# Moving later decay scans, one load and one pair of a fused Mamba2 and FFN kernel to other places in its head

## The chip, the cores and the metric

One core of one Trainium2 chip. The metric is the device time of one execution in microseconds (us), taken as the median of several; lower is better. Fast runs of one kernel in the same rounds differ by up to 1.4% here, so kernels are compared through several fast runs of the same rounds. A run counts as slow, and is left out, when it is over 1.5% above the fastest of its kernel.

## The reference

A chunked linear attention (Mamba2-SSD) is followed by a bilinear feed-forward layer. Cut to what matters:

```python
# x: (4, 8, 768, 32)  a: (4, 8, 768)  B, C: (4, 8, 768, 16)
for c in range(nc):                                   # chunks along the sequence
    cum = np.cumsum(la, axis=-1)                      # la = log(a) of the chunk
    L = np.exp(cum[..., :, None] - cum[..., None, :]) * causal
    M = np.einsum('bhin,bhjn->bhij', Cc, Bc) * L
    y[:, :, sl] = M @ xc + (Cc @ state) * np.exp(cum)[..., None]
    state = decay_full * state + sum(Bc * xc * decay_from_j)
# ... then, with x = y as (3072, 256), w_a and w_b (256, 1536), w_out (1536, 256):
return ((x @ w_a) * (x @ w_b)) @ w_out
```

## The kernel before

The kernel works on blocks of 128 positions (not 32) and on two of the four batches at a time, which gives 12 "pairs" p. For each pair it does, in this order: scaling of B and C by decay factors; a transposition of both on TensorE (`transposes`); the scores C Bᵀ (`scores`); the causal mask (`mask`); the value product with x (`pv`), copied by ScalarE to `X2T`; then six "units" (p, k2) of the feed-forward layer and the output product. A unit is eight matmuls over 128x256, a sixth of the 1536 columns.

The decay factors come from scans on VectorE (running products of `a`, one of six blocks each), whose reciprocals are put into `selr`; small fp32 matmuls then spread them over the partitions (`factors_mm`, four calls for a block; the profile shows each as two matmuls, so eight for a block and 40 for five blocks).

```python
def load_w(q3, which=(0, 1)):                 # one third of Wa and/or Wb: pieces of 256 KB
    for W, src in [((Wa, moe_w_a), (Wb, moe_w_b))[w] for w in which]:
        c = slice(q3 * KC, (q3 + 1) * KC)
        wd.append(nc.gpsimd.dma_start(W[:, :, c], ...))
def warmup(n, bank, cols=512):                # matmuls whose result nobody reads
    for _ in range(n):
        nc.tensor.matmul(bank[:, 0:cols], warm[:, 0:128], warm[:, 0:cols], ...)
def unit(p, k2):
    a_ps = psf.tile([128, 512], f32, name="aps", tag="ff")     # psf: 4 PSUM banks
    b_ps = psf.tile([128, 512], f32, name="bps", tag="ff")
    ...                                                         # 8 matmuls
    nc.scalar.copy(asb, a_ps)
    return lambda: nc.vector.tensor_tensor(out=s["hk"]..., in0=b_ps, in1=asb, op=ALU.mult)
def go(*items):
    for p, k2 in items:
        unit(p, k2)()
# --- loads, in the order of SyncE's queue (B, C, x are numbers 0, 1, 2) ---
load1(nc.sync, 1, 0, 0)
load1(nc.sync, 1, 1, 1)
load1(nc.sync, 1, 0, 1)
load1(nc.sync, 1, 1, 0)
load1(nc.sync, 1, 2, 0)
load1(nc.sync, 1, 2, 1)
load(2)
# --- GpSimd's software queue: three weight pieces early ---
load_w(0)
...                                           # the causal mask
load_w(1, (0,))
# --- head ---
warmup(6, SC[3])
scan(0, 1)
sel_over_mid(0, 1)
v = factors_mm(0, 1)
...
transposes(0, [tb, tcp], nc.vector.tensor_copy, lambda: warmup(2, SC[3], 128))
scores(0)
...
load_w(1, (1,))                               # the fourth weight piece, after pair 0's GpSimd mask
load_w(2)
...
warmup(5, tcp)
pv_u(0, 0, py, True)                          # pair 0's value product in two halves
...
scan(3, NBLK)
h = unit(0, 0)
turn(0)                                       # pair 0's states
sel_over_mid(1, NBLK)
h()
go((0, 1))
v = factors_mm(1, NBLK)                       # 40 small matmuls
...
transposes(1, None, nc.vector.tensor_copy)
h = unit(0, 2)
scores(1)
mask(product(1, 3), by_pool=True)
mask(product(1, 2))
h()
h = unit(0, 3)
mask(product(1, 0))
scale_x(1, nc.scalar)
...                                           # gps: the products for the carried state
mask(product(1, 1))
h()
go((0, 4))
pv(1)
state(0)
state(1)
go((0, 5), (1, 0), (1, 1), (1, 2))
transposes(2)
go((1, 3))
h = unit(1, 4)
scores(2)
...
```

The schedule is manual: the profile shows the instructions of each engine in the order in which the program names them (on GpSimd the fourth weight piece is issued at 8.96 us, behind pair 0's mask at 7.86).

## Time and profile before

| | before |
|---|---|
| median of three runs | 130.52 us (130.06 to 130.95) |
| span of the profiled run | 128.0 us, mean granted TensorE clock 0.999 |
| TensorE busy | 118.6 us, 93% of the span |
| TensorE continuous | from about 25 us to the end, 9.03 us a pair |
| landing of pair 1's B and C, last halves | 11.8 and 12.3 us |
| landing of the fourth and last weight piece of Wa, Wb | 14.9 and 18.7 us |
| scores of pair 2 on TensorE | 26.93 us, with 11 units done |

To read it: in this kernel all work of TensorE from the scores of pair 2 onward is a fixed string without holes. So the start of those scores, put at equal work (0.87 us for each unit that is done more or less), is a gauge for the whole time. A matmul over 256 columns starts every 0.11 us at full clock (0.87 us for the eight of a unit, from 21.31 to 22.18 in the kernel before); in the timeline a group of four then spans 0.60 us.

### The profile page before, as it was taken

The page shows a single profiled execution, that of the slowest core. Times are in us where ns is not written, and L with a number is a line of the kernel's source. Part 1 is how long each engine was busy: PE and PEld are TensorE (multiplying, and loading weights), DVE is VectorE, ACT ScalarE, POOL GpSimd, SP SyncE. Part 2 cuts the span into 40 slices and gives each one's busy share as a digit, 9 for nine tenths or more (in the row PEclk, how much of TensorE's full clock was granted, in tenths as well). Part 3 has the DMA queues.
Part 4 walks back from the last instruction along what each step waited for, and adds up shares of the span by engine and source line. Part 5 has one row for each costly group of instructions (what it writes and reads, how often), then busy time and mean ns, then how long its engine had stood idle before and what let it go on. Part 6 is the DMA issues. An engine that isn't in the chain of part 4 may idle for free.

```text
span 128.0 us, 4399 instructions
## 1 busy us (share of the span) xinstructions
PE 118.6 (93%) x1761; PEld 97.1 (76%) x1761; DVE 89.6 (70%) x178; ACT 66.5 (52%) x129; POOL 62.0 (48%) x106
## 2 busy tenths in 40 slices
PE   6969979799999999999999999999999999999960
PEld 2425757688887888888888888888888888888840
DVE  4676769658695976967958959959759569364420
ACT  3344567594836545455556456465445464564410
POOL 7966830799982925907828447338339100000000
PEclk9999999999999999999999999999999999999999
DMA  3999999775435666566456555565565310211203
GB/s 66 158 215 164 211 199 216 117 136 111 105 67 88 156 90 111 120 110 142 91 96 146 104 87 131 111 111 123 101 133 116 73 42 0 46 41 23 51 8 82
DMA packets 51555, 13.76 MB, mean 107 GB/s; under 512 B 45328, under 2 KB 51504, under 8 KB 51536
## 3 DMA queue, kind: packets, MB, share of 16 engines
q1 hardware_dynamic: 46560, 10.72, 43.8%
q0 software_dynamic: 3184, 2.36, 12.5%
q10 hardware_dynamic: 1792, 0.41, 1.6%
q8 instruction: 13, 0.21, 0.7%
q14 instruction: 6, 0.05, 0.1%
HBM read 11.13 MB, written 3.15 MB: 111 GB/s over the span
## 4 chain that ended last, share of the span: by engine, by line
PE 77%; DMA 9%; SPq 7%; POOL 1%; issue 1%; ACTq 1%; DVE 0%; POOLq 0%
PE ops L493 25%; PE aps L476 22%; PE bps L476 21%; DMA cn<-in_C_dram 9%; SPq L123 7%; PE SC L380 3%; PE SC L336 3%; PE SC L397 2%; ACTq L123 1%; POOL bm L262 1%; PE SC L313 0%; POOL cm L262 0%; DVE osb L506 0%; POOLq L451 0%; POOLq L262 0%
## 5 line engine op out<-in xcount | busy, mean ns | idle before, releaser
L486 DVE TENSOR_TENSOR hk<-bps,asb 128x512 f16<-128x512 f32 x72 | 49.2, 687 | 20.8 <-ACT asb L485 18.9
L485 ACT COPY asb<-aps 128x512 f32<-128x512 f32 x72 | 42.1, 587 | 17.9 <-PE aps L476 16.4
L476 PE MATMUL bps<-X2T,Wb 128*128 128x256 f16 x288 | 43.2, 273 | 1.1 <-ACT G L611 1.1
L476 PE MATMUL aps<-X2T,Wa 128*128 128x256 f16 x288 | 43.5, 273 | 0.1
L493 PE MATMUL ops<-Wo,hk 128*128 128x256 f16 x288 | 35.3, 273 | 0.0
L476 PEld LDWEIGHTS <-Wb 128*128 128x128 f16 x288 | 28.1, 98 | 4.5 <-issue 0.6
L493 PEld LDWEIGHTS <-hk 128*128 128x128 f16 x288 | 27.4, 98 | 4.1
L476 PEld LDWEIGHTS <-Wa 128*128 128x128 f16 x288 | 26.8, 98 | 4.8 <-issue 0.3
L370 DVE TENSOR_TENSOR t<-SC,causal 128x512 f16<-128x512 f32 x45 | 29.4, 681 | 1.3 <-ACT tmp L367 1.0
L451 POOL TENSOR_TENSOR sbd<-U,maskbd 128x512 f16<-128x512 f32 x10 | 11.5, 1154 | 21.1 <-DVE U L447 21.0
L508 ACT ACTIVATE osb<-ops 128x256 f32<-128x256 f32 x23 | 8.8, 383 | 23.6 <-PE ops L493 22.9
L249 POOL TENSOR_SCALAR x<-xn 128x512 f16<-128x512 f32 x9 | 13.4, 1489 | 0.8 <-DMA xn<-in_x_dram 0.2
L408 ACT ACTIVATE X2T<-SC 128x512 f16<-128x512 f32 x11 | 6.6, 597 | 5.1 <-PE SC L380 5.1
L262 POOL TENSOR_TENSOR bc<-cn,fC 128x128 f16<-128x128 f32 x16 | 6.1, 402 | 5.6 <-DMA cn<-in_C_dram 3.4
L262 POOL TENSOR_TENSOR t<-bn,fB 128x256 f16<-128x256 f32 x12 | 7.7, 639 | 0.1
L262 POOL TENSOR_TENSOR bc<-bn,fB 128x128 f16<-128x128 f32 x16 | 6.1, 401 | 0.0
L380 PEld LDWEIGHTS <-x 64*32 64x32 f16 x384 | 3.2, 91 | 3.2 <-ACT x L247 1.6
L201 PE MATMUL SC<-warm 128*128 128x512 f16 (+1 forms) x14 | 4.4, 453 | 1.2 <-DVE warm L150 1.2
L427 DVE STREAM_TRANSPOSE dt<-SC 128x64 f32<-128x64 f32 x9 | 2.2, 249 | 4.1 <-ACT X2T L408 4.1
L262 POOL TENSOR_TENSOR cm<-cn,fC 128x128 f16<-128x128 f32 (+1 forms) x5 | 2.1, 445 | 5.9 <-DMA cn<-in_C_dram 5.9
L368 POOL TENSOR_TENSOR t<-tmp,causal 128x512 f16<-128x512 f32 x3 | 3.5, 1156 | 3.1 <-ACT tmp L367 3.1
L380 PE MATMUL SC<-t,x 64*32 64x144 f16 (+1 forms) x352 | 4.8, 224 | 0.0
(69 smaller groups left out, 66.8 us busy)
## 6 DMA issues: line engine op xcount, KB each, us to landing
xn<-in_x_dram SPq DMA_DIRECT2D x23, 128.0 KB, 3.2
out_dram<-osb SPq DMA_DIRECT2D x46, 64.0 KB, 2.1
bn<-in_B_dram SPq DMA_DIRECT2D x23, 64.0 KB, 2.7
cn<-in_C_dram SPq DMA_DIRECT2D x23, 64.0 KB, 3.3
Wa<-in_moe_w_a_dram POOLq DMA_DIRECT2D x3, 256.0 KB, 6.8
Wb<-in_moe_w_b_dram POOLq DMA_DIRECT2D x3, 256.0 KB, 6.6
Wo<-in_moe_w_out_dram POOLq DMA_DIRECT2D x1, 768.0 KB, 10.2
xn<-in_x_dram ACTq DMA_DIRECT2D x1, 128.0 KB, 5.4
```

The costliest lines, as they stand in the source:

```text
L123: return eng.dma_start(pair_in[p][which][64 * bt : 64 * bt + 64].rearrange("i h r n -> i h (r n)"), src.rearrange("h (i r) n -> i h (r n)" ...
L249: eng.tensor_scalar(xo, xi, XS, None, ALU.mult)
L262: return eng.tensor_tensor(out=out, in0=i0, in1=i1, op=ALU.mult)
L370: nc.vector.tensor_tensor(out=o_, in0=i_, in1=c_, op=ALU.mult)
L380: nc.tensor.matmul(py[bt][32 * g : 32 * g + 32, u * (Q + N) : u * (Q + N) + w], s["X16"][k, h, r, :], s["T1"][k, h, r, 0:w], start=(first ...
L408: nc.scalar.activation(out=X2T[:, p].rearrange("p u t q -> p t u q"), in_=s["PY"][:, :, :, 0:Q], func=AF.Copy, scale=YS / XS,)
L451: nc.gpsimd.tensor_tensor(out=Sbd.rearrange("p t (h d) -> p t h d", h=H), in0=U32[:, p].unsqueeze(2).broadcast_to((128, 2, H, D)), in1=mas ...
L476: nc.tensor.matmul(ps[:, kk * 2 * Q : (kk + 1) * 2 * Q], W[:, f, k * 128 : (k + 1) * 128], X2T[:, p, f].rearrange("p t q -> p (t q)"), sta ...
L485: nc.scalar.copy(asb, a_ps)
L486: return lambda: nc.vector.tensor_tensor(out=s["hk"][:, 2 * k2 : 2 * k2 + 2, :].rearrange("p k q -> p (k q)"), in0=b_ps, in1=asb, op=ALU.mult)
L493: nc.tensor.matmul(o_ps[:, 0:d_model], hk[:, k, bt * Q : (bt + 1) * Q], Wo[:, k, :], start=(k == 0), stop=(k == NK - 1), skip_group_check= ...
L508: nc.scalar.activation(out=o_sb, in_=o_ps[:, 0:d_model], func=AF.Copy, scale=1.0 / (YS * YS))
```

## The change

Its intent is to take the waits of the head away. Three parts:

1. **Scans and factors early.** The scans of blocks 1 to 5 move ahead, and the 40 factor matmuls go into places where TensorE waited or ran warm-up matmuls: 16 between pair 0's transposes, 24 before pair 0's value product. Five of 23 warm-ups go (two of 128 columns, three of 512). Scaling pair 1's C goes from GpSimd to VectorE, some memsets change engines. Three small products for the carried state (`hr`, `hs`, `hsx`) and one `selr` go from VectorE to GpSimd, a copy of pair 0 from VectorE to ScalarE, and the causal mask is made ahead of the first weight piece.
2. **Loads.** The fourth weight piece is issued directly behind the third. x of pair 1 leaves SyncE's queue for GpSimd's software queue: one half behind the fourth weight piece, one ahead of the last two.
3. **Pair order.** Pair 1's value product and units (1,0) to (1,3) run ahead of (0,4) and (0,5), which need the last weights. The matmul `gps` for the carried state moves behind (1,0).

```diff
-    load1(nc.sync, 1, 2, 0)
-    load1(nc.sync, 1, 2, 1)
...
+    load_w(0)
+    load_w(1)
+    load1(nc.gpsimd, 1, 2, 0)
...
-    transposes(0, [tb, tcp], nc.vector.tensor_copy, lambda: warmup(2, SC[3], 128))
-    scan(2, 3)
+    transposes(0, [tb, tcp], None, lambda: factors_mm(fps[:, W1 : 3 * W1], 1, 3))
+    scan(3, NBLK)
...
-    load_w(1, (1,))
+    load1(nc.gpsimd, 1, 2, 1)
     load_w(2)
-    scale_bc(1, 1, nc.gpsimd)
...
-    warmup(5, tcp)
+    warmup(1, tcp)
+    factors_mm(fps3[:, 0 : 3 * W1], 3, NBLK)
+    warmup(1, tcp)
...
-    scan(3, NBLK)
     h = unit(0, 0)
     turn(0)
-    sel_over_mid(1, NBLK)
     h()
+    scale_bc(1, 1, nc.vector)
     go((0, 1))
-    v = factors_mm(1, NBLK)
...
-    go((0, 4))
     pv(1)
+    turn(1)
+    go((1, 0))
+    ...                                       # gps and its copy
+    go((1, 1))
     state(0)
     state(1)
-    go((0, 5), (1, 0), (1, 1), (1, 2))
+    go((1, 2), (1, 3))
     transposes(2)
-    go((1, 3))
-    h = unit(1, 4)
+    go((0, 4))
+    h = unit(0, 5)
     scores(2)
```

More of the change, by code (lines that the diff above doesn't have):

```diff
@@ L146 @@
     load1(nc.sync, 1, 1, 0)
-    load1(nc.sync, 1, 2, 0)
-    load1(nc.sync, 1, 2, 1)
     load(2)
     nc.vector.memset(warm.bitcast(u32), 0)
+    nc.vector.memset(headm, 1.0)
     nc.vector.memset(zero, 0.0)
-    for t_ in bc:
-        nc.vector.memset(t_[:, 0:4].rearrange("p k h n -> p (k h n)").bitcast(u32), 0)
+    nc.vector.memset(ident, 1.0)
+    nc.vector.memset(causal, 1.0)
     nc.gpsimd.memset(sel, 1.0)
@@ L163 @@
     )
-    nc.gpsimd.memset(headm, 1.0)
     for sign, base in ((1, 0), (-1, N - 1)):
@@ L177 @@
     )
-    nc.gpsimd.memset(ident, 1.0)
     nc.gpsimd.affine_select(
@@ L188, in load_w @@
             wd.append(nc.gpsimd.dma_start(W[:, :, c], src.rearrange("(f p) e -> p f e", p=128)[:, :, c]))
-    load_w(0)
-    nc.gpsimd.memset(causal, 1.0)
     for bt in range(2):
@@ L196 @@
         )
-    load_w(1, (0,))
+    load_w(0)
+    load_w(1)
+    load1(nc.gpsimd, 1, 2, 0)
     def warmup(n, bank, cols=512):
@@ L208, in scan, with sel_over_mid @@
             nc.vector.tensor_tensor_scan(Pr[:, k], a_sb[:, k], zero, 1.0, ALU.mult, ALU.add)
-    def sel_over_mid(lo, hi):
+    def sel_over_mid(lo, hi, eng=None):
         nc.vector.reciprocal(rmid[:, lo:hi], Pr[:, lo:hi, 63])
-        nc.vector.tensor_tensor(
+        (eng or nc.vector).tensor_tensor(
             out=selr[:, lo:hi].rearrange("p k t c -> p k (t c)"),
@@ L217, in sel_over_mid, with factors_mm @@
         )
-    def factors_mm(lo, hi):
-        fps = psf.tile([128, 512], f32, name="fps", tag="ff")
-        F = fps[:, 0 : (hi - lo) * 2 * NBP * H].rearrange("p (k r c) -> p k r c", k=hi - lo, r=2)
+    def factors_mm(fps, lo, hi):
+        F = fps.rearrange("p (k r c) -> p k r c", k=hi - lo, r=2)
         for k in range(lo, hi):
@@ L233, in factors_mm @@
                     )
-        return F.rearrange("p k r c -> p (k r c)")
     def flat(f, lo, hi):
@@ L537 @@
     sel_over_mid(0, 1)
-    v = factors_mm(0, 1)
-    nc.vector.reciprocal(flat(fB, 0, 1), v)
-    nc.scalar.copy(flat(fC, 0, 1), v)
+    W1 = 2 * NBP * H
+    fps = bank("fps")
+    factors_mm(fps[:, 0:W1], 0, 1)
+    scan(1, 3)
+    nc.vector.reciprocal(flat(fB, 0, 1), fps[:, 0:W1])
+    nc.scalar.copy(flat(fC, 0, 1), fps[:, 0:W1])
     warmup(2, SC[3])
@@ L543 @@
     scale_bc(0, 0, nc.vector)
+    sel_over_mid(1, 3)
     n1 = scale_bc(0, 1, nc.vector)
-    scan(1, 2)
     tb, tcp = bank("tb"), bank("tc")
-    transposes(0, [tb, tcp], nc.vector.tensor_copy, lambda: warmup(2, SC[3], 128))
-    scan(2, 3)
+    transposes(0, [tb, tcp], None, lambda: factors_mm(fps[:, W1 : 3 * W1], 1, 3))
+    nc.scalar.copy(flat(fC, 1, 3), fps[:, W1 : 3 * W1])
+    scan(3, NBLK)
     warmup(1, SC[3])
@@ L553 @@
     tc.add_manual_dep(n0.ins, n1.ins.name, AFTER, reason="C first")
+    sel_over_mid(3, NBLK, nc.gpsimd)
     mask(product0(1, 1), by_pool=True)
@@ L565 @@
     nc.gpsimd.tensor_copy(maskbd, headm.unsqueeze(2).broadcast_to((128, H, D)))
+    for t_ in bc:
+        nc.gpsimd.memset(t_[:, 0:4].rearrange("p k h n -> p (k h n)").bitcast(u32), 0)
     n0 = load(3)
     tc.add_manual_dep(n0[0].ins, wd[5].ins.name, AFTER, reason="weights first")
-    warmup(5, tcp)
+    fps3 = bank("fps")
+    warmup(1, tcp)
+    factors_mm(fps3[:, 0 : 3 * W1], 3, NBLK)
+    nc.scalar.copy(flat(fC, 3, NBLK), fps3[:, 0 : 3 * W1])
+    warmup(1, tcp)
     py = st[0]["py"] = [bank("py0"), bank("py1")]
@@ L579 @@
     warmup(1, tcp, 128)
-    scan(3, NBLK)
     h = unit(0, 0)
     turn(0)
-    sel_over_mid(1, NBLK)
     h()
+    scale_bc(1, 1, nc.vector)
     go((0, 1))
-    v = factors_mm(1, NBLK)
-    nc.vector.tensor_tensor(out=hr, in0=Pr[:, 0:NG, Q - 1], in1=rmid[:, 0:NG], op=ALU.mult)
-    nc.vector.tensor_tensor(out=hs, in0=hr, in1=Pr[:, 1:NBLK, 63], op=ALU.mult)
-    nc.vector.tensor_tensor(
-        out=hsx,
-        in0=hs.unsqueeze(1).broadcast_to((BH, nb, NG)),
-        in1=selb.rearrange("p (b g) -> p b g", b=nb),
-        op=ALU.mult,
-    )
     transposes(1, None, nc.vector.tensor_copy)
-    nc.scalar.copy(flat(fC, 1, NBLK), v)
     h = unit(0, 2)
@@ L606 @@
     load(4)
+    mask(product(1, 1))
+    h()
+    nc.gpsimd.tensor_tensor(out=hr, in0=Pr[:, 0:NG, Q - 1], in1=rmid[:, 0:NG], op=ALU.mult)
+    nc.gpsimd.tensor_tensor(out=hs, in0=hr, in1=Pr[:, 1:NBLK, 63], op=ALU.mult)
+    nc.gpsimd.tensor_tensor(
+        out=hsx,
+        in0=hs.unsqueeze(1).broadcast_to((BH, nb, NG)),
+        in1=selb.rearrange("p (b g) -> p b g", b=nb),
+        op=ALU.mult,
+    )
+    scale_bc(2, 1, nc.gpsimd)
+    scale_bc(2, 0, nc.gpsimd)
+    tail(2, nc.gpsimd)
+    pv(1)
+    turn(1)
+    go((1, 0))
     gps = bank("gps")
@@ L611 @@
     nc.scalar.copy(G.rearrange("p b g -> p (b g)"), gps[:, 0 : nb * NG])
-    mask(product(1, 1))
-    h()
-    scale_bc(2, 1, nc.gpsimd)
-    scale_bc(2, 0, nc.gpsimd)
-    tail(2, nc.gpsimd)
-    go((0, 4))
-    pv(1)
+    go((1, 1))
     state(0)
     state(1)
-    go((0, 5), (1, 0), (1, 1), (1, 2))
+    go((1, 2), (1, 3))
     transposes(2)
-    go((1, 3))
-    h = unit(1, 4)
+    go((0, 4))
+    h = unit(0, 5)
     scores(2)
@@ L628 @@
     scale_x(2, nc.scalar)
-    h2 = unit(1, 5)
+    h2 = unit(1, 4)
     mask(product(2, 1))
+    h()
     mask(product(2, 2))
-    h()
+    h2()
+    go((1, 5))
     out_half(0, 0)
-    h2()
     scale(3)
```

## The prediction

> **What bounds the kernel now.** I read the page's busy slices first, then the chain that ended last, then the four-window table, and only then the PE timeline of the head. The slices:
>
> ```profile
> PE   6969979799999999999999999999999999999960
> DMA  3999999775435666566456555565565310211203
> PE 77%; DMA 9%; SPq 7%; POOL 1%; issue 1%; ACTq 1%; DVE 0%; POOLq 0%
> ```
>
> A slice is 3.2 us. TensorE has holes only in the first eight slices and the last two; the DMA engines are full in slices 2 to 7. The chain is loads for its first part and TensorE afterwards. The window table (core; us, then busy us and instructions of each engine, clock, DMA) says the same in numbers:
>
> ```profile
> 0.00:10.80 10.80, 8.16 (x99) 3.62 (x100) 5.87 (x18) 4.10 (x9) 8.47 (x22) 1.00 0.93 153
> 10.80:25.10 14.30, 11.95 (x189) 9.28 (x188) 11.61 (x30) 7.96 (x17) 6.59 (x12) 1.00 1.24 183
> 25.10:123.60 98.50, 98.48 (x1479) 84.16 (x1476) 71.74 (x131) 54.22 (x104) 46.93 (x74) 1.00 0.47 94
> ```
>
> From 25.10 to 123.60 us PE is idle for 0.02 us. In the chain, the first 12-matmul group of a pair starts at 62.07, 71.10, 80.12, 89.15 and 98.18: 9.03 us a pair. So whatever the change does, it can only pay in the head, by letting PE do more of its fixed work before the place where it becomes continuous. The head on PE (start, busy us, operation, count, wait):
>
> ```profile
> 10.82 0.80 PE L476 MATMUL aps<-X2T,Wa 128*128 128x256 f16 x4
> 12.17 0.60 PE L476 MATMUL aps<-X2T,Wa 128*128 128x256 f16 x4
> 13.21 1.38 PE L225 MATMUL fps<-selr,Pr 32*64 32x16 f32 x40
> 16.17 0.43 PE L336 MATMUL SC<-ct,bt 32*64 32x128 f16 x32 [0.38 <-DVE ct L323]
> 17.86 0.60 PE L476 MATMUL aps<-X2T,Wa 128*128 128x256 f16 x4
> 19.52 0.60 PE L476 MATMUL bps<-X2T,Wb 128*128 128x256 f16 x4 [1.06 <-ACT G L611]
> 20.05 0.45 PE L380 MATMUL SC<-t,x 64*32 64x144 f16 x32
> 24.86 0.28 PE L313 MATMUL SC<-ident,bm 128*128 128x128 f16 x2 [0.77 <-POOL bm L262]
> 26.93 0.43 PE L336 MATMUL SC<-ct,bt 32*64 32x128 f16 x32
> ```
>
> I call the eight matmuls of one pair and one sixth of the columns a unit; (0,4) is pair 0, sixth 4. Units (1,0), (1,1), (1,2) start at 21.31, 22.18, 23.05: 0.87 us each. Time lost between 10.82 and 25.10: about 0.5 before (0,1) at 12.17 (its bank is held until VectorE turns pair 0's states, which stands behind three scans, 10.98 to 12.01); 1.4 for the 40 factor matmuls; 0.5 before pair 1's scores at 16.17; 1.2 inside (0,4) between 18.30 and 19.52; 0.9 before pair 2's transposes at 24.86. Sum 4.5 us. That is the most that the change can win here.
>
> [...] So I use start spacing. [...] 0.87 us / 8 = 109 ns. [...] loads of x issued at 7.9 to 10.3 us land 7.2 and 9.1 us later, where the shortest of that kind takes 2.9. So putting x of pair 1 on GpSimd's queue changes its place, not its cost.
>
> **The change part by part.** Durations are those of the rows of before.
>
> 1. *Scans and factor products.* 16 of the 40 factor matmuls go between pair 0's transposes, 24 before pair 0's value product. PE runs warm-up work or waits there now: it waits 1.13 us until 9.41 for x of pair 0, whose scaling starts on ScalarE at 8.72. 24 x 34.5 ns = 0.83 us. GpSimd makes their weights after VectorE's last early reciprocal, near 7.7, so they run about 8.1 to 8.9. This just fits. The cost: scans, reciprocals and selr delay pair 0's masks by some 0.5 us (VectorE 7.21 to 7.75, done 9.65), but the first product needs only two of the three, done near 9.05. As the weights' issue starts 0.7 us later (masks are made first), x of pair 0 may come a little earlier. I put unit (0,0) at 10.6, before 10.82. The scans being gone from 10.98, (0,1) follows directly, near 11.6 to 12.5, before 12.17 to 13.04. With the factor products gone, transposes of pair 1 may start at 12.6, before 14.52. Gain so far 1.9 us.
>
> 2. *Pair 1's C on VectorE.* Scaling C (0.41 us) moves behind pair 0's first product hk (0.65 us from 11.95): 12.6 to 13.0. GpSimd does B right after the weights' issue, 11.8 to 12.5; B's last half landed at 11.8, C's at 12.3 before. So C's transposes start near 13.05: 0.3 us lost on PE. Then two ScalarE copies (0.84), one VectorE copy (0.29): scores of pair 1 near 14.15, if unit (0,2) between them is not held up.
>
> 3. *Weights.* Landings of the six weight pieces before: 8.1, 9.8, 12.0, 14.9, 16.8, 18.7 (issue plus time to landing); 1.7 to 2.2 us apart except where the fourth was issued only at 8.96. Now four are issued back to back from about 3.0: estimated 8.5, 10.3, 12.3, 14.2. (0,2) wants the fourth at 13.6. I charge 0.5 us: scores at 14.7. Then x of pair 1: two pieces of 128 KB, an estimate of about 1 us each, so 16.3, before 18.7.
>
> 4. *Pair 1 ahead of the last weights.* Scores to value product took 16.17 to 20.05 before, and VectorE's part (wait for ScalarE's tmp, mask, hk, two masks) ends at 19.85 whatever PE does. The same row of VectorE stands in the changed order, so 3.7 us again: value product at 18.4. But now PE has only (0,3) to do in it: 0.37 + 0.87 us. A **new hole of about 2.5 us**. After the value product PE wants pair 1's X2T at once: 0.15 + 0.60 + 0.05 us after its 0.37, another hole of 0.8; before, (0,5) ran there. So (1,0) starts at 18.4 + 0.37 + 0.8 = 19.6. Then (1,0), gps (0.3), (1,1) to (1,3) until 23.4, transposes 0.23, (0,4) and (0,5) until 25.4, scores of pair 2. The wait for the last weights (18.7 before, now about 20, wanted at 23.6) is gone. The wait for C of pair 2 is gone as well: SP has two loads fewer ahead of it, so it should land near 17, before 23.2.
>
> *Sum.* Scores of pair 2: 25.4 with 10 units done; before 26.93 with 11. At equal work 25.4 + 0.87 = 26.3, a gain of 0.65 us; 1.15 if the fourth weight piece is not waited for. Removed 4.5 + 0.2, newly lost 0.3 + 0.5 + 2.5 + 0.8 = 4.1. All behind it is continuous PE work and keeps its 98.5 us.
>
> **Rivals.** *All of it is won.* If the two new holes were filled, the gain would be 3.5 to 4 us: 126.5 to 127. For it: all four old waits are really attacked. Against: in the changed order no PE work stands between (0,3) and the value product, nor between that and (1,0). *Loads eat it.* The weights now share one first-in, first-out queue with x; if x of pair 1 lands after 18, or the fourth weight piece after 15, each us later costs one us: 130.5 to 131.5. For it: the DMA engines are full until 23 us and the bytes stay the same. Against: x had 2.4 us to spare in my row, and C of pair 2 leaves the path. *VectorE becomes the bound* after pair 1, with four state updates of 0.19 us between hk's: at 0.7 us per hk against 0.87 per unit it catches up; 0.3 us at most. *The clock halves* in the 2.5 us hole: [...] I see no sign of it in the trace with 1.1.
>
> **Range and chances.** 130.5 - 0.8 (between 0.65 and 1.15) = 129.7. The three runs before spread 0.9 us. Both holes filled by luck of earlier landings would give 128.6; late loads 130.7. Over 2% needs 2.6 us of the 4.7 at stake, and the 3.3 us of structural holes stand against that: 0.04. Slower by 2% needs a late load chain of over 3 us: 0.02.
>
> **What would show it.** Right: no factor matmuls after 10 us; (0,1) directly behind (0,0); pair 1's scores at 14 to 15; a PE hole of 2 to 2.5 us before pair 1's value product, ended by VectorE's mask, and one of 0.8 behind it, ended by ScalarE's X2T; no PE wait for weights after 20 or for C of pair 2; continuous PE with the same 9.03 us a pair; a span near 127.2. Wrong: the hole ended by DMA x or ScalarE x, unit (0,2) waiting over 1 us for the fourth weight piece, or the hole much shorter because pair 1's masks come faster than 3.7 us after its scores.

## The result and the profile after

The changed kernel takes **135.01 us** (134.31 to 136.96, four runs) against 130.74 us (130.06 to 131.14, four runs) for the one before. The ratio is 1.032, with a 95% interval from 1.025 to 1.039: slower, outside the predicted range. A ratio here always compares the fast runs of two kernels from the same rounds, so it is not quite the ratio of the medians. One of the changed kernel's runs was slow and is not in the ratio.

The page of the changed kernel, with the busy tenths of TensorE, its granted clock in tenths, and the engines' shares of the chain that ended last:

```profile
PE   6897195899999999999999999999999999999970
PEclk9999757779999999999999999999999999999999
DMA  3899999864038467555645646557555420120213
PE 77%; DMA 10%; DVE 5%; ACT 2%; issue 1%; ACTq 1%; SPq 0%; DVEq 0%
```

A slice is 3.3 us. Before, the clock row was 9 throughout; now it drops in slices 5 to 9 and TensorE is almost idle in slice 5, where it had been at 9. Behind slice 9 all is as it was. The window table has, after the window, its length and then busy us (and instructions) of TensorE, weight loads, VectorE, ScalarE and GpSimd, the granted clock, the DMA share and GB/s:

```profile
10.80:25.10 14.30, 8.70 (x110) 5.65 (x109) 6.18 (x14) 5.47 (x10) 7.92 (x17) 0.76 1.29 192
17.00:19.00 2.00, 2.00 (x26) 1.22 (x32) 0.88 (x3) 1.43 (x3) 1.40 (x4) 0.50 1.23 206
25.20:28.20 3.00, 3.00 (x15) 2.09 (x15) 1.60 (x5) 0.90 (x3) 0.00 (x0) 0.50 0.50 104
```

Between 10.8 and 25.1 us TensorE did 110 matmuls in 8.70 busy us; before it did 189 in 11.95. Two stretches have exactly half the clock while TensorE is busy without a break. The timeline of TensorE (start, us, operation, count, and the idle time before it with what ended it) names the places:

```profile
10.58 0.80 PE L471 MATMUL aps<-X2T,Wa 128*128 128x256 f16 x4
11.65 0.60 PE L471 MATMUL aps<-X2T,Wa 128*128 128x256 f16 x4
15.90 0.40 PE L308 MATMUL SC<-ident,bm 128*128 128x128 f16 x2 [3.21 <-POOL bm L257]
16.79 0.39 PE L308 MATMUL SC<-ident,cm 128*128 128x128 f16 x2 [0.49 <-DVE cm L257]
16.97 1.06 PE L471 MATMUL aps<-X2T,Wa 128*128 128x256 f16 x4
18.82 0.65 PE L331 MATMUL SC<-ct,bt 32*64 32x128 f16 x32
22.19 0.24 PE L375 MATMUL SC<-t,x 64*32 64x144 f16 x4 [0.91 <-POOL hsx L605]
22.70 0.43 PE L375 MATMUL SC<-t,x 64*32 64x144 f16 x28 [0.26 <-DVE t L365]
23.84 0.60 PE L471 MATMUL aps<-X2T,Wa 128*128 128x256 f16 x4 [0.71 <-ACT X2T L403]
26.92 1.06 PE L471 MATMUL aps<-X2T,Wa 128*128 128x256 f16 x4
31.44 0.43 PE L331 MATMUL SC<-ct,bt 32*64 32x128 f16 x32
```

Up to 12.5 us this is what was predicted: (0,0) at 10.58, (0,1) at 11.65, no factor products between. Then pair 1's transposes wait 3.21 us for B, whose scaling on GpSimd had itself waited for its load; what follows runs at half clock (1.06 us for four matmuls at 16.97). The value product is at 22.70, then comes the hole of 0.71, and unit (1,2) at 26.92 is at half clock again. The hole of 0.91 is put down to `hsx` on GpSimd, but VectorE's mask of the first heads ended within 0.1 us of it (21.37 plus half of 1.28 us for two): the releaser is inferred, and the mask is as likely.

The time can be added up at equal work in this one profiled run, against the run before. The first step also contains the first stretch at half clock, from about 14.5 to 21.5 us, whose own cost no run separates:

| place | before | after | step |
|---|---|---|---|
| value product of pair 1 (its main part) | 20.05 | 22.70 | +2.65 |
| units of pair 0 done by then | 5 | 4 | +0.87 |
| hole behind it | none | 0.71 | +0.71 |
| half clock behind it | none | about 3.4 us | about +1.7 |
| wait for pair 2's B and C | 0.77 | none | -0.77 |
| sum of the rows above | | | +5.2 |
| scores of pair 2, at equal work | 26.93 | 31.44 + 0.87 | +5.38 |

The 1.7 is from this trace: (1,0) to (1,3) with `gps` took 5.53 us (23.84 to 29.37), where four units of 0.87 and 0.35 for `gps` make 3.83. The spans differ by 5.5 us (133.5 and 128.0). So three things have to be explained: the late B and C, the holes, and the half clock. The DMA queues from 8 to 12 us (packets, MB, share of 16 engines' time; q0 is the software queue with the weights, q1 SyncE's), before:

```profile
DMA packets 2625, 0.72 MB, mean 181 GB/s; under 512 B 2189, under 2 KB 2625, under 8 KB 2625
q0 software_dynamic: 468, 0.45, 78.4%
q1 hardware_dynamic: 2156, 0.28, 50.8%
```

And after:

```profile
DMA packets 1596, 0.84 MB, mean 210 GB/s; under 512 B 896, under 2 KB 1590, under 8 KB 1596
q0 software_dynamic: 739, 0.74, 107.9%
q1 hardware_dynamic: 857, 0.11, 28.4%
```

More bytes moved, but SyncE's queue, with B and C of pair 1, got 857 small packets in place of 2156. Their last halves landed at 15.2 and 15.9 us; the prediction had taken over 11.8 and 12.3.

### The profile page after: what moved, and what is told of

It is laid out like the page before. It is cut to its first block, busy times and chain, and to the rows that moved or that the text cites.

```text
span 133.5 us, 4393 instructions
## 1 busy us (share of the span) xinstructions
PE 121.6 (91%) x1756; PEld 98.8 (74%) x1756; DVE 89.6 (67%) x177; ACT 67.1 (50%) x131; POOL 63.9 (48%) x110
## 4 chain that ended last, share of the span: by engine, by line
PE 77%; DMA 10%; DVE 5%; ACT 2%; issue 1%; ACTq 1%; SPq 0%; DVEq 0%
PE ops L488 24%; PE aps L471 22%; PE bps L471 22%; DMA cn<-in_C_dram 10%; PE SC L375 3%; PE SC L331 3%; DVE hk L481 2%; PE SC L392 2%; DVE t L365 1%; ACT asb L480 1%; DVE U L440 1%; DVE cm L257 1%; ACTq L123 1%; ACT x L242 0%; PE SC L308 0%
## 5 line engine op out<-in xcount | busy, mean ns | idle before, releaser
L471 PE MATMUL aps<-X2T,Wa 128*128 128x256 f16 x288 | 45.3, 281 | 0.7 <-ACT X2T L403 0.7
L471 PE MATMUL bps<-X2T,Wb 128*128 128x256 f16 x288 | 44.9, 280 | 0.4 <-ACT asb L480 0.4
L471 PEld LDWEIGHTS <-Wb 128*128 128x128 f16 x288 | 29.0, 101 | 4.6 <-issue 0.5
L471 PEld LDWEIGHTS <-Wa 128*128 128x128 f16 x288 | 27.6, 100 | 5.8 <-issue 0.9
L446 POOL TENSOR_TENSOR sbd<-U,maskbd 128x512 f16<-128x512 f32 x10 | 11.6, 1156 | 23.8 <-DVE U L442 19.6
L503 ACT ACTIVATE osb<-ops 128x256 f32<-128x256 f32 x23 | 8.8, 384 | 24.5 <-PE ops L488 22.9
L244 POOL TENSOR_SCALAR x<-xn 128x512 f16<-128x512 f32 x9 | 13.4, 1491 | 2.6 <-DMA xn<-in_x_dram 2.1
L198 PE MATMUL SC<-warm 128*128 128x512 f16 (+1 forms) x12 | 3.9, 472 | 1.3 <-DVE headm L149 1.3
L317 ACT ACTIVATE bt<-SC,par 128x256 f16<-128x256 f16 x6 | 2.5, 471 | 4.4 <-PE SC L308 4.3
## 6 DMA issues: line engine op xcount, KB each, us to landing
xn<-in_x_dram SPq DMA_DIRECT2D x21, 128.0 KB, 3.5
xn<-in_x_dram POOLq DMA_DIRECT2D x2, 128.0 KB, 8.4
```

Source lines behind the costliest of these rows:

```text
L244: eng.tensor_scalar(xo, xi, XS, None, ALU.mult)
L446: nc.gpsimd.tensor_tensor(out=Sbd.rearrange("p t (h d) -> p t h d", h=H), in0=U32[:, p].unsqueeze(2).broadcast_to((128, 2, H, D)), in1=mas ...
L471: nc.tensor.matmul(ps[:, kk * 2 * Q : (kk + 1) * 2 * Q], W[:, f, k * 128 : (k + 1) * 128], X2T[:, p, f].rearrange("p t q -> p (t q)"), sta ...
L503: nc.scalar.activation(out=o_sb, in_=o_ps[:, 0:d_model], func=AF.Copy, scale=1.0 / (YS * YS))
```

## The experiments

Fifteen kernels; all gave the right result. Each has its own runs of the kernel before in the same rounds. The questions were: does the fourth weight piece or x of pair 1 delay B and C; what does the clock cost; what does each of the three parts do alone; what do the dropped warm-ups do.

### The fourth weight piece late (a_w1b_late)

```diff
 # against the changed kernel
-    load_w(1)
+    load_w(1, (0,))
     load1(nc.gpsimd, 1, 2, 0)
...
+    load_w(1, (1,))
     load1(nc.gpsimd, 1, 2, 1)
```

> The changed kernel with one edit: the fourth weight piece (Wb, second third) is issued after pair 0's GpSimd mask, as before the change, instead of straight behind the third. Theory A ([...] B and C of pair 1 land at 15.2 and 15.9 us instead of 11.8 and 12.3): they land before 13.5 us, the 3.2 us TensorE hole before pair 1's transposes shrinks under 1 us, the first half-clock stretch goes, time 129.5 to 131.5. Rival B (B and C are late because SP's own later loads were issued earlier, or because of x of pair 1 in the software queue): they still land after 15 us, time 134 to 136.

Theory A was that the early fourth piece on the software queue makes B and C of pair 1 late; rival B, that SyncE's own later loads or x of pair 1 do. 133.27 us; ratio to before 1.0246 (1.0186 to 1.0306), against 1.0319 for the changed kernel. B and C landed at 13.2 and 13.7. TensorE's timeline:

```profile
13.89 0.28 PE L308 MATMUL SC<-ident,bm 128*128 128x128 f16 x2 [1.02 <-POOL bm L257]
16.10 0.61 PE L471 MATMUL bps<-X2T,Wb 128*128 128x256 f16 x4 [1.19 <-DMA Wb<-in_moe_w_b_dram]
```

The wait for B falls from 3.21 to 1.02 us, and 1.19 comes back as a wait for the very piece that was postponed. In these two profiles the early fourth piece makes up 2.0 of the 3.4 us that B came later, and 2.2 of the 3.6 for C; it is not the reason for most of the loss. The time lies above theory A's range. Landings scatter: the six profiles of kernels of this family with the piece early have B at 13.6 to 15.2 us, the six with it late at 12.1 to 13.2.

### x of pair 1 back on SyncE's queue (a_x_sp)

```diff
 # against the changed kernel
+    load1(nc.sync, 1, 2, 0)
+    load1(nc.sync, 1, 2, 1)
...
-    load1(nc.gpsimd, 1, 2, 0)
...
-    load1(nc.gpsimd, 1, 2, 1)
```

> The changed kernel with x of pair 1 back on SP's queue behind pair 1's B and C, weights as in the change. Theory A: x is not the cause, because in the software queue it stood behind the fourth weight piece; B and C of pair 1 still land near 15 us and the hole stays over 2.5 us, time 133.5 to 137 (x of pair 1 comes later, near 19 us or after). Rival B: B and C land before 13 us and the time falls to 131 or less.

134.91 us, ratio 1.0375 (1.032 to 1.043): no gain. B and C landed at 13.7 and 14.7 in the profiled run, yet the half clock behind pair 1's value product lasted from 21.6 to 28.2 us. That is 6.6 us, twice as long as in the changed kernel. x's place does not explain the loss.

### Warm-ups in the first hole (a_filler)

```diff
 # against the changed kernel
+    warmup(15, SC[3])
     transposes(1, None, nc.vector.tensor_copy)
```

> The changed kernel with 15 more warm-up matmuls (about 3.2 us at full clock) between unit (0,1) and pair 1's transposes, that is in the hole. It measures the clock's part alone. Theory A with the clock as a second loss: TensorE clock stays 1.00 from 12 to 21 us, landings are as in the changed kernel, the second half-clock stretch (25.2 to 28.2) may stay, time 1 to 2.5 us less than the changed kernel: 132.5 to 134. Rival C (the half clock costs nothing as TensorE waits anyway): time within 0.5 us of the changed kernel.

136.56 us, ratio 1.0487 (1.0416 to 1.0557): a miss. In its profile the matmuls ran at half rate until about 13.4 us, so the fifteen began only at 14.85 in place of about 12.5. They took 3.40 us, as planned, and ended at about 18.1, behind the landing of C at about 15. They delayed the work that they should have kept warm, and the half clock from 24.5 to about 30.5 stayed. That told me two things: the second stretch belongs to the holes at the value product, and the head is not always warm.

### The fourth weight piece early in the kernel before (b_w1b_early)

```diff
 # against the kernel before
-    load_w(1, (0,))
+    load_w(1)
...
-    load_w(1, (1,))
```

> The kernel before with only the fourth weight piece moved up: issued straight behind the third. Theory A: C of pair 1 lands 1.5 to 3.5 us later than 12.3, the factor matmuls of before hide part of it, TensorE gets a hole of 1 to 2 us before pair 1's transposes; time 131 to 134. Rival B: landing within 0.5 us of before, time within 1 us of 130.7.

130.27 us, ratio 1.0013 (0.9952 to 1.0075). C landed at about 13.2, a full us later than before, and the time did not change: a miss for theory A. In the profile the 40 factor products (12.47 to 13.85) hide part of the delay, and TensorE then waits 0.72 us for B; the transposes start at 14.57, as before (14.52), because this head was 0.66 us earlier ((0,0) at 10.16). The small loads also suffered less here. From 8 to 12 us SyncE's queue moved 1855 packets, about as many as with the late piece, and not the 828 to 1005 of the early piece in the changed kernel's family (see c_w1b). Why the piece costs them so much more in that family, where it is issued at 5.20 and not at 5.92, no run tells.

### Loads as before, new pair order kept (a_dma_back)

```diff
 # against the changed kernel
+    load1(nc.sync, 1, 2, 0)
+    load1(nc.sync, 1, 2, 1)
...
-    load_w(1)
-    load1(nc.gpsimd, 1, 2, 0)
+    load_w(1, (0,))
...
-    load1(nc.gpsimd, 1, 2, 1)
+    load_w(1, (1,))
```

> The changed kernel with the whole order of loads of before (fourth weight piece after pair 0's mask, x of pair 1 on SP's queue); the early scans and the pair order of the change stay. Theory A2 (two losses: late B and C of pair 1 through the software queue, and the hole of 2.5 + 0.8 us around pair 1's value product, which also takes the clock to half for about 3 us): B and C land at 12 to 13 us as before, the first hole is under 1 us, but the hole before the value product (now held by x of pair 1 near 19 us) and a half-clock stretch behind it stay: 131.5 to 134. Rival D (loads alone explain the loss): 129 to 130.5.

134.28 us, ratio 1.0333 (1.0277 to 1.0388): as large a loss as the changed kernel's, without any of the new loads, and a little more than theory A2 allowed. Its timeline around the value product:

```profile
21.23 0.24 PE L376 MATMUL SC<-t,x 64*32 64x144 f16 x4 [1.77 <-POOL hsx L606]
21.73 0.43 PE L376 MATMUL SC<-t,x 64*32 64x144 f16 x28 [0.26 <-DVE t L366]
22.87 0.60 PE L472 MATMUL aps<-X2T,Wa 128*128 128x256 f16 x4 [0.71 <-ACT X2T L404]
24.60 1.03 PE L472 MATMUL aps<-X2T,Wa 128*128 128x256 f16 x4
25.43 1.06 PE L472 MATMUL bps<-X2T,Wb 128*128 128x256 f16 x4
27.05 0.60 PE L472 MATMUL bps<-X2T,Wb 128*128 128x256 f16 x4
```

Holes of 1.77, 0.26 and 0.71 us with one value product between them, then half clock from about 23.5 to 26.9.

### The same with warm-ups in that hole (a_dma_back_filler)

```diff
 # against a_dma_back
+    warmup(9, bank("wm"))
     pv(1)
```

> The same with nine more warm-up matmuls (1.9 us at full clock) in the hole before pair 1's value product. It measures the clock alone: the hole is longer than 2 us, so they delay nothing. Theory A2: no half-clock stretch after 20 us and 1 to 2 us less than without them. Rival C (the half clock is harmless): within 0.5 us of the run without them.

132.54 us (132.16 to 133.43) against 134.28 (133.59 to 135.12) in the same rounds: **1.74 us less**, from nine matmuls that compute nothing. With four runs of each the difference of the means is 1.65 us, give or take about 1. Ratio to before 1.0205 (1.0158 to 1.0253).

```profile
17.74 2.11 PE L199 MATMUL wm<-warm 128*128 128x512 f16 x9
20.18 0.43 PE L376 MATMUL SC<-t,x 64*32 64x144 f16 x28 [0.16 <-DVE t L366]
21.32 0.60 PE L472 MATMUL aps<-X2T,Wa 128*128 128x256 f16 x4 [0.71 <-ACT X2T L404]
22.61 0.61 PE L472 MATMUL aps<-X2T,Wa 128*128 128x256 f16 x4
27.80 0.43 PE L332 MATMUL SC<-ct,bt 32*64 32x128 f16 x32
```

The hole of 0.71 is still there, the clock stays full behind it. So the half clock is a consequence of the hole before the value product. Its price is best read behind the value product, where the two profiles run the same work: from (1,0) to pair 2's transposes took 5.49 us at half clock (22.87 to 28.36) and 4.12 without (21.32 to 25.44), 1.4 us less. The rest of the difference between the two profiles lies in the head, which ran at half rate until 16.6 us in the first and until 14.2 in the second. The holes themselves remain.

### Scans alone (a_scans_only) and new loads without the new order (a_order_back)

```diff
 # both against the changed kernel; a_scans_only has the loads of a_dma_back as well
+    go((0, 4))
     pv(1)
     turn(1)
-    go((1, 0))
+    go((0, 5))
...
-    go((1, 1))
+    go((1, 0))
     state(0)
     state(1)
-    go((1, 2), (1, 3))
+    go((1, 1), (1, 2))
     transposes(2)
-    go((0, 4))
-    h = unit(0, 5)
+    go((1, 3))
+    h = unit(1, 4)
...
```

> The first part of the change alone: early scans and factor products, pair 1's C on VectorE, masks first; loads and the order of the pairs as before. Theory A2: the factor products are really gone from TensorE's path, so this is 0 to 1.2 us faster than before: 129.3 to 130.7, with TensorE waiting for weights and x of pair 1 in their place. Rival E (the first part itself costs, through ScalarE's and VectorE's longer early work): 131 or more.

> The changed kernel with only the pair order of before: unit (0,4) ahead of pair 1's value product, (0,5) behind it. Theory A2: B and C of pair 1 stay late (14 to 16 us) and so does the first hole, but the second hole is filled by the two units: 1.5 to 3 us less than the changed kernel, 132 to 133.5. Rival D: within 0.7 us of the changed kernel, 134.3 to 135.7.

In both, `gps` stays behind the value product, where the change put it. Early scans and factors alone: 130.46 us, ratio 1.0028 (0.9969 to 1.0087), so the same. New loads with the old order: 131.54 us, ratio 1.0118 (1.0071 to 1.0165), a little under theory A2's range. The first three are from the same rounds, the changed kernel from its own, so the table has the ratios to the kernel before beside the medians:

| | old pair order | new pair order |
|---|---|---|
| loads as before | 130.46, 1.0028 (a_scans_only) | 134.28, 1.0333 (a_dma_back) |
| new loads | 131.54, 1.0118 (a_order_back) | 135.01, 1.0319 (changed kernel) |

By the ratios the order costs 3.1% or 4.0 us (2.0% or 2.6 us in the lower row), the new loads 0.9% or 1.2 us in the left column and nothing that can be told from noise in the right one.

The profiles narrow this down. The programs of a row are the same up to the scores of pair 1. From there to the scores of pair 2, at equal work, the new order takes 2.3 us more in the upper row (18.05 to 30.64 with one unit fewer, 15.74 to 26.86) and 2.8 in the lower (18.82 to 31.44 with one fewer, 17.48 to 28.18). What is left of the difference between two profiles of a row (2.3 and 1.3 us) lies ahead of the scores, where the order cannot matter: the head of a_dma_back, for one, was at half rate until 16.6 us, that of a_scans_only was not.

Why early scans gain nothing is in the timeline of a_scans_only:

```profile
12.93 0.28 PE L309 MATMUL SC<-ident,bm 128*128 128x128 f16 x2
15.20 0.61 PE L472 MATMUL bps<-X2T,Wb 128*128 128x256 f16 x4 [1.17 <-DMA Wb<-in_moe_w_b_dram]
18.27 0.61 PE L472 MATMUL bps<-X2T,Wb 128*128 128x256 f16 x4 [0.68 <-DMA Wb<-in_moe_w_b_dram]
23.72 0.28 PE L309 MATMUL SC<-ident,bm 128*128 128x128 f16 x2
25.73 0.60 PE L472 MATMUL aps<-X2T,Wa 128*128 128x256 f16 x4 [0.75 <-DVE hk L482]
26.86 0.43 PE L332 MATMUL SC<-ct,bt 32*64 32x128 f16 x32
```

Pair 1's transposes start at 12.93 in place of 14.52: the 1.6 us are won. 1.17 go to the fourth weight piece, 0.68 to a later one. At pair 2's transposes 1.1 us are there again (23.72 before 24.86), because the wait for pair 2's B is gone, but now VectorE is behind and holds a bank for another 0.75, and the scores of pair 2 are at 26.86 against 26.93.

### The fourth piece early with scans alone, and C on another queue (c_w1b, c_act, c_act_warm)

```diff
 # c_w1b against a_scans_only
-    load_w(1, (0,))
+    load_w(1)
...
-    load_w(1, (1,))
 # c_act, on top of c_w1b
+    load1(nc.scalar, 1, 1, 1)
+    load1(nc.scalar, 1, 1, 0)
...
-    load1(nc.sync, 1, 1, 1)
-    load1(nc.sync, 1, 1, 0)
 # c_act_warm, on top of c_act: one more warm-up at three places
```

> Early scans with the loads and pair order of before, and only the fourth weight piece moved straight behind the third. In the run without that move TensorE waited 1.17 us for this piece in unit (0,2). Theory A2: that wait goes, but C of pair 1 lands about 1 us later, as it did when the same move was made in the kernel before (13.3 against 12.3), so little is won: 129.3 to 130.7. Rival F (the weight wait is the last thing between the early scans and a gain): 128.5 to 129.3.

131.71 us, ratio 1.0129 (1.0048 to 1.021), slower than both theories said. B and C landed at 15.1 and 15.6, where a_scans_only had them at 12.2 and 12.4. TensorE waited 1.96 us for B, and behind that wait the clock was at half from 16.1 to about 19.4 us. DMA from 8 to 12 us in a_scans_only:

```profile
q0 software_dynamic: 496, 0.48, 76.3%
q1 hardware_dynamic: 2144, 0.33, 55.7%
```

and in c_w1b:

```profile
q0 software_dynamic: 721, 0.70, 104.6%
q1 hardware_dynamic: 1005, 0.13, 31.4%
```

One `dma_start` at another place, issued at 5.19 us in place of 9.64, reproduces the shift that the changed kernel shows. In the changed kernel's family the six profiles with the early piece have 721 to 748 packets on q0 and 828 to 1005 on q1 (the changed kernel, a_x_sp, a_filler, a_filler2, a_order_back, c_w1b), and the six with the late one 463 to 552 and 1858 to 2394 (a_w1b_late, a_dma_back, a_dma_back_filler, a_scans_only, a_order_w1b, d_state). The exception is b_w1b_early, outside that family: 643 and 1855 with the early piece. In the family, then, SyncE's queue, whose packets are small (0.11 MB in 857 in the changed kernel, about 130 bytes each), moved fewer of them, and the software queue with packets of about 1 KB (0.74 MB in 739) moved more. The load of C that is issued between 6 and 8 us, 64 KB, took 10.1 us to land in c_w1b and 6.8 in a_scans_only. In what order the DMA engines serve the two queues, no run shows. I tried a third queue for C:

> The same, with both halves of C of pair 1 issued on ScalarE's queue, behind x of pair 0, and no longer on SP's. Theory G [...]: with two queues of small loads B and C of pair 1 land by 12 us although the fourth piece is early; scores of pair 1 before 15 us; 128.8 to 130.2. Rival H (what counts is the total of bytes, not the queue): B or C still lands after 13 us, time as the run before it.

131.61 us, ratio 1.014 (1.0053 to 1.0227): a miss. Theory G was that with C on a queue of its own both B and C land by 12 us; rival H, that B or C still lands after 13. C's first half landed early, at 10.8 (14.1 in c_w1b), but B at 15.0. ScalarE's queue moved 495 packets from 8 to 12 us and SyncE's fell from 1005 to 694: together only 18% more. The edit also held up ScalarE's first copies (TensorE waited 1.05 us for one at 6.8), so pair 0's start moved. What sets the landing stays open.

> The same with three more warm-up matmuls in the gaps before 9 us. In two of eight profiles of the changed kernel's family the clock went to half near 7.4 us until 14, in two it had not risen before 13 to 16; in those the head was 1 to 2 us later. Theory I (tiny factor products in place of warm-up matmuls let the clock fall): no half clock in the head in the profile and a tighter spread, median 0.3 to 1 us less than without them. Rival: no change of the median beyond 0.3 us[...].

131.44 us, ratio 1.0104 (1.001 to 1.0198). The head's clock was full in its profile from about 6 us on, and the median moved by 0.17 us, inside the spread. Its profile has something else to teach:

```profile
15.39 0.28 PE L309 MATMUL SC<-ident,bm 128*128 128x128 f16 x2 [1.70 <-POOL bm L258]
16.28 0.29 PE L309 MATMUL SC<-ident,cm 128*128 128x128 f16 x2 [0.60 <-DVE cm L258]
16.41 0.60 PE L472 MATMUL aps<-X2T,Wa 128*128 128x256 f16 x4
```

Here TensorE was busy for 0.70 us in 3.0 (13.5 to 16.5), and the clock stayed at 1.00 in the window table. In a_dma_back it was busy for 0.81 us in 2.9 (20.1 to 23.0), and the clock halved at about 23.5. So close holes do not halve the clock each time.

### Warm-ups before the value product of the changed kernel (a_filler2)

```diff
 # against the changed kernel
+    warmup(9, bank("wm"))
     pv(1)
```

> The changed kernel itself with nine more warm-up matmuls (1.9 us at full clock) before pair 1's value product; everything else as in the change. With the loads of before these took 1.7 us off (134.28 to 132.54). Theory A2: 1 to 2 us less than the changed kernel, 133 to 134; at half clock, after the first hole, the nine take 3.8 us and may delay the product, which makes the gain smaller. Rival C: 134.5 to 135.5.

135.03 us (133.22 to 135.84), ratio 1.0327 (1.0205 to 1.0448): inconclusive. Two of four runs were slow. The two fast ones took 133.22 and 134.83; the first is the profiled one and has no half clock behind 20 us, but matmuls at half rate until about 16. In that profile the second stretch is gone as in a_dma_back_filler; whether the time fell by it this run cannot show, as the head's own clock differs from run to run by as much.

### Old order, late fourth piece, x left in the software queue (a_order_w1b)

The edits of a_order_back and a_w1b_late together.

> The changed kernel with the pair order of before and the fourth weight piece after pair 0's mask; x of pair 1 stays in the software queue. It leaves early scans and x in the software queue alone. Theory A2 (pair order costs 3.5 us, the early fourth piece about 1, the place of x nothing): 130 to 131, like the run with the loads of before (130.46). Rival J (x in the software queue costs as well): 131.2 or more.

130.07 us over five rounds, ratio **1.0001** (0.9964 to 1.0037). It keeps the early scans and x of pair 1 in the software queue. So these two cost nothing and gain nothing together with the old order, and the loss lies in the order and the fourth piece. Against a_order_back the late piece is worth 1.5 us (131.54 and 130.07, of different rounds).

### The same five warm-ups fewer in the kernel before (b_less_warm)

```diff
 # against the kernel before
-    transposes(0, [tb, tcp], nc.vector.tensor_copy, lambda: warmup(2, SC[3], 128))
+    transposes(0, [tb, tcp], nc.vector.tensor_copy)
...
-    warmup(5, tcp)
+    warmup(2, tcp)
```

> The kernel before with three full and two short warm-up matmuls fewer in its head (between pair 0's transposes, and behind its scores), about as many as the change dropped; nothing else. Theory I (in the change tiny factor products stand where warm-up matmuls kept the clock up): the clock falls in the head in some runs, median 0.5 to 2 us more than before. Rival K (they do nothing by then[...]): within 0.4 us of before.

130.99 us, ratio 1.0091 (1.005 to 1.0132): 1.2 us more, for five matmuls that compute nothing taken out of waits: inside theory I's range. Its page says that the clock was full throughout (the clock row is 9 in all 40 slices), and its timeline that it was not:

```profile
11.17 1.06 PE L476 MATMUL aps<-X2T,Wa 128*128 128x256 f16 x4
12.02 1.06 PE L476 MATMUL bps<-X2T,Wb 128*128 128x256 f16 x4
12.87 1.06 PE L476 MATMUL aps<-X2T,Wa 128*128 128x256 f16 x4
```

The half rate is not recorded here, where the kernel ran at it from 4.56 us at the latest (three full warm-ups in 1.14 us) until 13.8. The length of the groups has to be read as well. What the five did is less sure than the time: the three full warm-ups at 4.56 us already took 1.14 us (0.86 in the kernel before), and the first of the five would have come at 5.68. So the missing ones cannot be why the clock had not risen by then; they may be why it did not rise until 13.8.

### Scans alone, more warm-ups, pair 1's state later (d_state)

```diff
 # against a_scans_only; also one more warm-up at three places
     go((1, 0))
     state(0)
-    state(1)
     go((1, 1), (1, 2))
...
     state(2)
+    state(1)
```

> Early scans with loads and pair order of before (130.46 us), three more warm-up matmuls, and pair 1's state update on VectorE moved behind pair 2's. In the trace of that run TensorE waited 0.75 us for VectorE's product hk near 25 us and a third of a us on either side of it, which gave back the 1.1 us that pair 2's transposes had gained. Theory L (the gain of the early scans is given back to VectorE's queue there): 129.0 to 130.2, no wait over 0.3 us near 25 us. Rival M (weights and x bind, not VectorE): 130.2 to 131.

130.85 us over six runs, three of which were slow; the fast ones (130.31, 130.17, 129.11) have a ratio of 0.9989 (0.9934 to 1.0044), the same as before. The bank wait of 0.75 us near 25 us is gone as intended, but the scores of pair 2 were at 27.41 in that profile:

```profile
16.03 1.00 PE L472 MATMUL bps<-X2T,Wb 128*128 128x256 f16 x4 [1.48 <-DMA Wb<-in_moe_w_b_dram]
18.37 1.06 PE L472 MATMUL bps<-X2T,Wb 128*128 128x256 f16 x4
```

After a wait of 0.43 us for C (to 13.84) and 0.72 us of work the fourth weight piece was waited for by 1.48 us, and behind that wait the clock was at half until about 19.5. So removing one wait more did not move the end; what the bank wait alone is worth, this run does not tell. No version tried beats the kernel before.

## Why the prediction was wrong

**Up to 12.5 us it was right.** (0,0) was put at 10.6 and (0,1) at 11.6, and they came at 10.58 and 11.65. The factor products fitted into the waits. Some of it was luck with the clock: a_filler, the same program up to there, ran at half rate and had (0,0) at 12.75.

**Step 4 failed, in one term: the clock.** The sizes of the holes were right: 2.5 us were predicted before the value product, and where the clock before it was full they measured 1.77 + 0.26 (a_dma_back, a_x_sp, a_w1b_late); 0.8 behind it measured 0.71 there and in the changed kernel. The predicted 3.7 us from the scores to the value product were 3.9. What failed is the rival that I put aside in a sentence. That a hole of 2.5 us would leave the clock at full was my estimate: in the head of the trace before, the longest wait behind the first matmul was 1.13 us. The runs show that separate shorter holes can be enough: in a_dma_back TensorE had 0.81 us of work in the 2.9 us from 20.1 to 23.0, and the clock halved at about 23.5 and came back at about 26.9. That is 3.4 us at half rate (1.06 us for four matmuls in place of 0.60); half of it, 1.7 us, is the most that it can cost. The traces give 1.4 to 1.7 us for it and the medians with and without fillers 1.74; in a_x_sp it lasted 6.6 us. When close holes halve the clock and when they do not (c_act_warm), these runs do not settle. Of the 4.1 us "newly lost" in the sum of the prediction, this term is missing whole.

**The same step counted its gains from the wrong kernel.** The pair order was to remove the waits for the last weights and for pair 2's C, 1.2 and 0.9 us in the kernel before. With the scans early and the old order (a_scans_only) these were already 0.68 and 0. The 1.2 us in the kernel before were not the weights' alone, either: they had landed at 18.7, and the wait until 19.52 was ended by ScalarE's copy `G` (19.31), which stood behind the scaling of x (18.77 to 19.40). The order had little left to win, and its two holes were paid in full. Between the two pairs' scores it cost 2.3 us in the profiles (a_dma_back and a_scans_only): 1.4 for the clock and 1.77 + 0.71 for the holes, less 0.68 and 0.75 of waits in a_scans_only, makes 2.45 by calculation.

**Step 2 failed, for a reason that lies in step 3.** B's and C's landings were taken over from before (11.8 and 12.3) while step 3 put 256 KB ahead in time into a stretch in which the DMA engines were busy (from 8 to 12 us their row is 9 in 37 of 40 slices before and in all 40 after). The estimates of step 3 for its own loads were good: the fourth piece landed at 14.4 (14.2 predicted), x of pair 1 at 16.8 at the latest (16.3). On the software queue the loads landed in the order of their issue: the fourth piece, the two halves of x and the last two pieces at 14.4, 15.6, 16.8, 17.6 and 19.4. What was not counted was whose time they took: from 8 to 12 us that queue's share rose from 78.4% to 107.9%, and SyncE's fell from 50.8% to 28.4%. B and C came at 15.2 and 15.9 us, and TensorE waited 3.21 us. The rival "loads eat it" had about the right size (0.8 to 1.8 us above the forecast) and the wrong victims. The cost, from three pairs of kernels that differ in that piece alone, each by its ratio to the kernel before since they ran in different rounds: 0.7% (changed kernel and a_w1b_late), 1.2% (a_order_back and a_order_w1b), 1.0% (c_w1b and a_scans_only), which is 0.9 to 1.5 us. The intervals of the first and the last pair overlap, so it is the three together that show it; in the kernel before the same edit cost nothing (1.0013).

**Step 1 was right in its mechanism and its gain was not there to keep.** The transposes of pair 1 do start 1.6 us earlier with scans alone, and the end does not move (1.0028). The prediction added up waits as if each could be removed by itself. Behind each stood the next: the weights, then VectorE's bank.

**The dropped warm-ups were not priced.** The prediction treats them as work that TensorE can spare. In the kernel before, taking the five out cost 1.2 us (b_less_warm). How much of the changed kernel's loss this is stays open: its profiled run had full clock from about 4.5 to 14.5 us, four other profiles with the same head (a_filler, a_dma_back, a_filler2, a_order_w1b) ran at half rate until 13 to 16.6 us (in a_filler2 1.06 us for four matmuls over 256 columns in place of 0.60) while their clock was recorded as 1.00, and three added warm-ups moved c_act by 0.17 us.

**The rest held:** no wait for weights beyond 20 us, none for C of pair 2 (it landed near 20 us and not near 17, still in time), and the same 9.03 us a pair behind the head.

## What to carry to other kernels

Before moving work into a wait of TensorE or a wait to another place, add up the holes that stand close together: holes with little between them can act as one hole, and then cost another 1.4 to 1.7 us behind it (a_dma_back: 1.77, 0.26 and 0.71 us with one value product between them; twice that in a_x_sp's trace by the length of the stretch). They did not each time (c_act_warm: 1.70 and 0.60 us, and the clock stayed at 1.00). When a load is issued earlier into a stretch in which the DMA engines are busy throughout, list the loads that land in the same time and ask which of them gets later; in the changed kernel it was the small ones, B and C of pair 1 (15.2 and 15.9 us in place of 11.8 and 12.3), on which everything waited. Waits of a chain are not a sum to be won: take one away alone on the chip, and look at what the engines wait for next.
